# Attention, routing and experts on one core: rows transposed two jobs ahead into buffers of their own, fetched by SyncE; weight loads issued by ScalarE; low halves taken on VectorE

## The chip, the cores and the metric

One core of a Trainium2 chip. The metric is the device time of the whole program in microseconds (us). Three runs of the kernel before took 657.96 to 662.32 us, median 660.88 us. The profile is of one execution of 659.64 us, whose trace spans 657.9 us.

## The reference, cut to what matters

```
k_p, v_p = mean of 8 neighbouring keys / values           # 576 -> 72 per head
attn = softmax(q @ k_p.T / 8); x = (attn @ v_p) as [4608, 512]
logits = x @ w_gate;  e_idx = argmax(logits)              # one expert of 8 per row
gate_w = softmax(logits)[e_idx];  eom = sigmoid(x @ w_output_gate)
for e in range(8):
    out[rows of e] = gate_w * eom[:, e] * (relu(x[rows of e] @ w1[e]) @ w2[e])
```

w1[e] is 512 x 1024 and w2[e] 1024 x 512, all in fp32.

## The kernel before, in words

**Two halves.** The first half (to about 190 us) computes attention and routing, and scatters each row of x into a table `xs` in device memory that is ordered by expert. Its tail takes the first rows of expert 0 through the first layer (`hidden_chunk`, L613) and part of the second (`output_chunk`, L619). The second half (`experts`) runs the experts.

**Jobs and slots.** An expert's rows come in tiles (slots) of 128 rows. A job is 3 or 2 slots of one expert; an expert with a single tile has a job of 2 slots of which one is real (`single`, function `l1` with n = 0). How many jobs there are is read from a table at run time, so every engine runs the same nest (expert, trips of 3, pairs of 2) with `body` as its job. VectorE, ScalarE and GpSimd have it written out for all 8 experts (`loops`); TensorE has expert 0 written out and then a loop of 4 turns with two experts each (`looped`).

**Exact products.** An fp32 number is split into a high half (rounded) and a low half (the rest). x, the hidden layer and the weights are each held as high and low, and every product takes three matmuls. ScalarE takes each high half, and VectorE the low halves of the weights (`split`, L1059) and of the hidden layer (`low`, L1090). GpSimd takes the low half of x (`xl`, L1197).

**One job, engine by engine.** TensorE: first layer `l1` (8 chunks f of 128 hidden columns, 12 matmuls each, into 5 PSUM banks `p_h`, so chunk f waits until VectorE has read chunk f - 5), then second layer `l2` tile by tile into `p_y`. ScalarE: 4 DMAs that fetch the next job's rows (`fetch`, L860), then `hidden` (8 ReLUs, with a weight split behind some of them), then the high halves `xh` of the next job's rows (L979), then weight splits that are left (`rest`, `finish`). VectorE: the previous job's last output, `hidden`, then the transposes `turn` of the next rows in place in `xq` (L1047), then splits and the scaling of outputs `y` (L1079) in turn. GpSimd: `sc` and `dst` (gate values and output rows of the job), gathers of the row numbers two jobs ahead (`ahead`, L1180), `xl` of the next job's rows, then the scatters of the outputs (L1212). SyncE: the row fetch of job 1, then the 52 weight loads from m = 12 on (L884), each as soon as the piece that is 6 earlier in the ring `stage` has been split.

**What orders the next job's rows.** `xt`, the halves that TensorE reads, exists once: `xh` may begin when `l1` is over, and the next `l1` begins when `xl` is over (L913 in the code, semaphore `xl`). `xq` exists once too: the fetch of the next rows waits for `xl` of these.

**Weight splits.** Expert e + 1's pieces j = 4 to 7 (for e = 0 all 8) are split in e's first job, pieces j = 0 to 3 of e + 2 in e's last job (`plan`, `further`). In a first job each split stands behind one ReLU; in a job of one real tile two stand there (POS) and the rest after.

**Case of these inputs.** Expert 0 has jobs of 3, 3 and 2 slots (the first of them already begun in the first half), 1 a single tile, 2 one job of 3, 3 a pair, 4 has 3, 2 and 2, 5 has 3 and 3, 6 a single tile, 7 has 3, 3, 3 and 2: 16 jobs.

Of the kernel before, what the change touches and what calls it, by code (L numbers as in the profile page):

```python
# [22 lines left out]
P = 128  # L23
# [37 lines left out]
POS = (4, 6)  # L61

# [19 lines left out]
def attention_and_routing(ctx, tc, sh, qT, kT, v, wg, wst, xs):  # L82
# [599 lines left out]
def experts(st, nc, sh, wst, xs, out):  # L682
# [18 lines left out]
    names = ["l1", "tx", "l2", "xh", "xl", "hh", "hl", "y", "sc", "c", "x0", "x1", "x2", "t", "out", "wh", "wl", "on", "ad", "g", "pre", "xd", "x"]  # L701
# [149 lines left out]
    def fetch(eng, u, more, sem):  # L851
        def row(u):
            u = nc.s_assert_within(u, 0, R - 1, skip_runtime_bounds_check_because="there are at most 50 slots")
            return nc.values_load_multi_w_load_instructions(
                sh.at[0:1, bass.ds(u, 1)], [eng.engine], min_val=0, max_val=ZROW,
                skip_runtime_bounds_check_because="rows of the experts' tables")[1][0]

        def tiles(at, n):
            for h in range(4):
                eng.dma_start(xq[32 * h:32 * h + 32, 0:4 * n].bitcast(I32),  # L860
                              whole_rows(xs)[bass.ds(at, P * n), P * h:P * h + P].rearrange("(g t) f -> t g f", t=32)).then_inc(sem, LANDED // 4)

        with eng.If(more > 0):
            tiles(row(u), 3)
        with eng.Else():
            at, beside = row(u), row(u + 1)
            with eng.If(beside - at == P):
                tiles(at, 2)
            with eng.Else():
                tiles(at, 1)  # L870
# [3 lines left out]
    @blk.sync  # L874
    def _(eng):
        rows = table(eng)
        with eng.If(rows[E + 1] > 2):
            fetch(eng, WIDE, (counts(rows[0])[0] - 1) * 128 + (rows[0] & 128), q["xd"])
        for m in range(LOADED, 8 * E):
            if m == STAGES + EARLY:  # L880
                eng.wait_ge(q["xd"], LANDED)
            if m >= STAGES + EARLY:
                eng.wait_ge(q["wl"], m - STAGES + 1 - EARLY)
            eng.dma_start(sh.stage[m % STAGES], wst[m // 8][:, CHUNK * (m % 8):CHUNK * (m % 8 + 1)]).then_inc(LD[m % STAGES], 16)  # L884
# [88 lines left out]
    def _(eng):  # L973
        act = nc.scalar.activation

        def xh(u, k):
            _, turned, (high, _) = turned_rows(sh, k)
            eng.wait_ge(q["tx"], u + k + 1)
            act(high, turned, AF.Copy).then_inc(q["xh"], 1)  # L979

        def split(some):
            for e, j in some:
                m, s, hi, lo = piece(e, j)
                if m >= LOADED:
                    eng.wait_ge(LD[m % STAGES], 16 * ((m - LOADED) // STAGES + 1))
                act(hi, s, AF.Copy).then_inc(q["wh"], 1)  # L986

        def body(e, size, job, u, single, nth, more, last, late):
# [19 lines left out]
            def next_rows():  # L1008
                eng.wait_ge(q["xl"], u + size)
                fetch(eng, u + size, more, q["xd"])  # L1010

            if done is None:
                next_rows()
            else:
                with eng.If(done <= 0):
                    next_rows()
            eng.wait_ge(q["t"], ROWS)
            choose(eng, e, size, single, nth, hidden, hidden_one, split, done, late)
            xh(u + size, 0)
            xh(u + size, 1)  # L1020
            with eng.If(more > 0):
                xh(u + size, 2)
# [11 lines left out]
        with eng.If(rows[E + 1] <= 2):  # L1034
            fetch(eng, 0, rows[E + 1] & 1, q["x"])
        begin(eng, rows, ["xh", "hh"], lambda k: xh(0, k))
# [3 lines left out]
    def _(eng):  # L1040
        def turn(u, k, job):
            if isinstance(job, int):
                eng.wait_ge(q["x"], LANDED)
            else:
                eng.wait_ge(q["xd"], LANDED * job)
            x = turned_rows(sh, k)[0]
            nc.vector.transpose(x, x).then_inc(q["tx"], 1)  # L1047

        def turns(u, job, more):
            turn(u, 0, job)  # L1050
            turn(u, 1, job)
            with eng.If(more > 0):
                turn(u, 2, job)
# [31 lines left out]
        def body(e, size, job, u, single, nth, more, last, late):  # L1085
# [30 lines left out]
            def hidden_and_turns(some):  # L1116
                hidden(some)
                turns(u + size, job + 1, more)

            def turns_and_split(some):  # L1120
                turns(u + size, job + 1, more)
                split(some)

            if done is None:
                choose(eng, e, size, single, nth, hidden, hidden_one, split, done, late)
                turns(u + size, job + 1, more)
            else:
                choose(eng, e, size, single, nth, hidden_and_turns, None, turns_and_split, done, late)
            rest(eng, e, size, single, nth, split, 0, INIT + 1 if done is not None else 4, done, late)
            soon = SOON[size] if e else 0  # L1130
# [174 lines left out]
```

## Time and profile before

| | |
|---|---|
| median of 3 runs | 660.88 us (657.96 to 662.32) |
| the profiled execution | 659.64 us, of which its trace spans 657.9 us; mean granted clock 0.969 |
| TensorE (PE) busy | 593.5 us, 90% of the span |
| VectorE (DVE) busy | 351.0 us, 53% |
| ScalarE (ACT) busy | 262.6 us, 40% |
| GpSimd (POOL) busy | 286.6 us, 44% |
| moved by DMA | 100.97 MB, mean 153 GB/s |

Times in the rows are us from the span's start. A row of a timeline gives start, duration, engine, line, operation, output <- inputs and count; behind it, in brackets, the idle time of the engine just before and what ended it. "issue" there is a wait that ended with nothing that the profile shows. PEld is TensorE's weight load, SPq and ACTq are the queues that issue DMAs.

### The profile page before, as it was taken

The numbers are of one execution on the slowest core, as the hardware profiler recorded it, in microseconds if no ns is written. First come the engines' busy times: TensorE is split into PE (matmuls) and PEld (weight loads), VectorE is DVE, ScalarE is ACT, GpSimd is POOL, SyncE is SP. The second block draws the span as 40 slices with busy tenths as digits, with TensorE's granted clock in tenths as the row PEclk, the third lists the DMA queues.
The fourth block names the chain that finished last, engine by engine and source line by source line (L and its number), as shares of the span: only waits on it lengthen the run. The fifth ranks groups of instructions, "written<-read, shape, count | busy, mean of one in ns | idle before, by whom it ended". The sixth has DMA issues, their size and how long they took to land.

```text
span 657.9 us, 11957 instructions
## 1 busy us (share of the span) xinstructions
PE 593.5 (90%) x3543; PEld 539.7 (82%) x3544; DVE 351.0 (53%) x797; ACT 262.6 (40%) x694; POOL 286.6 (44%) x380
## 2 busy tenths in 40 slices
PE   0899999989894999879869999999999599999996
PEld 0798998878783989769668989989898498989895
DVE  5688899998767223577536513275135722222221
ACT  2788888787334212336334402154031411111110
POOL 3668889753626323255233324344231623223233
PEclk9999999999998899979969999999999889999998
DMA  8878889987468310648845710366105022111111
GB/s 257 271 221 291 289 293 348 331 279 243 173 173 302 94 47 31 211 134 252 228 132 162 235 57 28 88 139 213 58 12 146 29 63 62 43 49 39 36 37 40
DMA packets 48431, 100.97 MB, mean 153 GB/s; under 512 B 5931, under 2 KB 27819, under 8 KB 46432
## 3 DMA queue, kind: packets, MB, share of 16 engines
q1 hardware_dynamic: 22192, 66.64, 31.9%
q0 software_dynamic: 7792, 24.60, 11.1%
q10 hardware_dynamic: 18368, 8.92, 5.7%
q14 instruction: 59, 0.48, 0.3%
q8 instruction: 20, 0.33, 0.2%
HBM read 78.56 MB, written 25.49 MB: 158 GB/s over the span
## 4 chain that ended last, share of the span: by engine, by line
PE 61%; issue 3%; POOL 2%; DVE 2%; ACT 1%; DMA 1%; SPq 0%; DVEq 0%; POOLq 0%
PE p_h L922 33%; PE p_y L903 29%; POOL xt L1197 2%; DMA rows<-xs 1%; DVE w1b L1059 1%; DVE rows L1047 1%; DVE w2b L1059 0%; ACT w2a L986 0%; POOL rows L1180 0%; DVE rows L1079 0%; SPq L860 0%; DVE q_even L1103 0%; ACT xt L979 0%; ACT w2b L986 0%; POOL out L1212 0%
## 5 line engine op out<-in xcount | busy, mean ns | idle before, releaser
L994 ACT ACTIVATE ht<-p_h 128x384 fp32r<-128x384 f32 (+1 forms) x104 | 46.8, 450 | 270.0 <-PE p_h L922 269.9
L922 PE MATMUL p_h<-xt,w1b 128*128 128x384 f32 (+1 forms) x736 | 121.9, 329 | 16.8 <-issue 9.8
L922 PEld LDWEIGHTS p_h<-xt,w1b 128*128 128x128 f32 x736 | 120.6, 197 | 18.5 <-issue 18.0
L1090 DVE SCALAR_TENSOR_TENSOR ht<-p_h,ht 128x384 fp32r<-128x384 f32 (+1 forms) x104 | 52.6, 506 | 133.3 <-ACT ht L994 133.3
L903 PE MATMUL p_y<-w2b,ht 128*128 128x512 f32 x480 | 113.2, 396 | 0.0
L922 PE MATMUL p_h<-xt,w1a 128*128 128x256 f32 (+1 forms) x640 | 98.3, 316 | 13.3 <-POOL xt L1197 13.3
L922 PEld LDWEIGHTS p_h<-xt,w1a 128*128 128x128 f32 x640 | 97.4, 197 | 14.6 <-POOL xt L1197 9.2
L903 PEld LDWEIGHTS p_y<-w2b,ht 128*128 128x128 f32 x480 | 90.0, 188 | 21.0
L1212 POOL DMA_INDIRECT out<-rows,dst x41 | 41.5, 1013 | 123.1 <-DVE rows L1079 120.2
L903 PE MATMUL p_y<-w2a,ht 128*128 128x512 f32 x408 | 94.2, 390 | 0.4 <-PE p_y L619 0.4
L903 PEld LDWEIGHTS p_y<-w2a,ht 128*128 128x128 f32 x408 | 76.2, 188 | 16.3 <-issue 0.9
L1079 DVE TENSOR_SCALAR rows<-p_y,sc 128x512 f32<-128x512 f32 x41 | 30.4, 747 | 108.9 <-PE p_y L903 96.3
L1197 POOL TENSOR_TENSOR xt<-rows,xt 128x512 fp32r<-128x512 f32 x40 | 53.6, 1364 | 64.0 <-ACT xt L979 63.9
L261 ACT ACTIVATE p<-p_h,m 128x72 f32<-128x72 f32 x288 | 71.9, 373 | 21.9 <-DVE m L256 21.4
L278 PE MATMUL p_y<-vbd,pT 128*128 128x162 f32 (+1 forms) x480 | 74.0, 306 | 5.4 <-DVE xg L300 4.7
L278 PEld LDWEIGHTS p_y<-vbd,pT 128*128 128x128 f32 (+1 forms) x480 | 60.9, 179 | 9.0 <-DVE xg L300 4.1
L1180 POOL DMA_INDIRECT rows<-xs,src x51 | 54.6, 1071 | 24.7 <-POOL src L1176 14.3
L408 POOL DMA_INDIRECT xs<-xg,where x36 | 37.2, 1033 | 35.7 <-DVE grec L294 9.9
L191 POOL TENSOR_TENSOR kq<-kq 128x288 f32<-128x288 f32 (+1 forms) x63 | 40.6, 670 | 15.6 <-DMA kq<-kT 14.8
L250 PE MATMUL p_h<-kbd,q_even 128*128 128x144 f32 (+1 forms) x160 | 28.6, 306 | 15.4 <-DMA q_even<-qT 12.7
L271 ACT ACTIVATE pT<-ptr 128x384 f32<-128x384 f32 x72 | 38.7, 538 | 1.6 <-PE ptr L270 1.4
L270 PE MATMUL ptr<-ident,p 128*128 128x128 f32 x216 | 36.0, 276 | 1.0 <-DVE vbd L238 0.9
(165 smaller groups left out, 680.2 us busy)
## 6 DMA issues: line engine op xcount, KB each, us to landing
stage<-wst SPq DMA_DIRECT2D x64, 512.0 KB, 5.2
kq<-kT SPq DMA_DIRECT2D x7, 1152.0 KB
rows<-xs ACTq DMA_DIRECT2D x28, 192.0 KB
rows<-v SPq DMA_DIRECT2D x16, 288.0 KB
kq<-qT SPq DMA_DIRECT2D x4, 1152.0 KB
q_even<-qT SPq DMA_DIRECT2D x3, 1152.0 KB
xs<-xs SPq DMA_DIRECT2D x8, 320.0 KB
rows<-xs ACTq DMA_DIRECT2D x20, 128.0 KB
```

What stands on the lines that cost most here:

```text
L191: eng.tensor_tensor(k[:, :, 0:w], k[:, :, 0:w], k[:, :, w:2 * w], op=ALU.add)
L261: nc.scalar.activation(pt[i % 3][:, 4 * a + h, 0:KEYS], sv[:, h], AF.Exp, bias=m[:, h:h + 1])
L271: nc.scalar.activation(pT_t[i][:, 3 * a:3 * a + 3, :], tr[:, 0:384].rearrange("p (c n) -> p c n", c=3), AF.Copy)
L278: nc.tensor.matmul(av[r0:r0 + n, COLS * c:COLS * c + 2 * COLS], pT[:, 3 * a + c, r0:r0 + n], vbd[b % 2][:, a, c].rearrange("p h f -> p (h ...
L408: ins = nc.gpsimd.indirect_dma_start(out=whole_rows(xs), out_offset=bass.IndirectOffsetOnAxis(ap=where, axis=0), in_=x.bitcast(I32), in_of ...
L903: i = mm(to, ht[:, h, f, P * k:P * k + P], w[:, part, o:o + DM], start=(f == 0 and part == 0 and h == 0), stop=(f == 7 and h == 1))
L922: i = mm(to, w[:, part, o:o + P], x, start=(d == 0 and k == 0), stop=(d == 3 and k == len(terms) - 1))
L994: act(ht[:, 0, f, 0:size * P], p_h[f % DEEP][:, 0:size * P], AF.Relu).then_inc(q["hh"], 1)
L1090: nc.vector.scalar_tensor_tensor(ht[:, 1, f, 0:n], src, 0.0, ht[:, 0, f, 0:n].bitcast(F32), op0=ALU.max, op1=ALU.subtract).then_inc(q["hl" ...
L1180: nc.gpsimd.indirect_dma_start(out=xm[:, k].bitcast(I32), out_offset=None, in_=xs, in_offset=bass.IndirectOffsetOnAxis(ap=src[:, k:k + 1], ...
L1197: nc.gpsimd.tensor_tensor(low, turned, high.bitcast(F32), op=ALU.subtract).then_inc(q["xl"], 1)
L1212: nc.gpsimd.indirect_dma_start(out=out, out_offset=bass.IndirectOffsetOnAxis(ap=dst[:, k:k + 1], axis=0), in_=yb[2 if k == size - 1 else k ...
```

## The change

- Rows are transposed from `xq` into buffers `turned[0..2]` (two in SBUF, one in a PSUM bank that was the fifth of `p_h`; `l1` has 4 banks then). VectorE transposes for job j + 2 at the end of job j, ahead of `y`; always three tiles.
- SyncE fetches rows in a loop over all jobs of its own (`every_job`); the fetch of job j waits until the transposes of job j - 1 are done.
- ScalarE issues the weight loads: behind the split of piece m it waits until VectorE has split piece m - 2, and loads piece m + 4. It no longer fetches rows, and no longer waits for the row table (`t`) in each job.
- `xl` is VectorE's, behind `hidden`, in the second half and in `turn_x` of the first. All splits of a job and the transposes stand ahead of its `y`.

```
-        nc.gpsimd.tensor_tensor(low, turned, high.bitcast(F32), op=ALU.subtract)
+        nc.vector.tensor_tensor(low, turned, high.bitcast(F32), op=ALU.subtract)
...
-    p_h = sh.p_h + [psum(f"p_h{k}", [P, 512]) for k in (3, 4)]
+    p_h = sh.p_h + [psum("p_h3", [P, 512])]
+    turned = [sb(f"turned{k}", [P, 4, P], F32) for k in range(2)] + [psum("turned2", [P, 4, P])]
...
     @blk.sync
+            if job is not None:
+                eng.wait_ge(q["tx"], eng.to_reg(job * WIDE + 1))
+            for h in range(4):
+                eng.dma_start(xq[32 * h:32 * h + 32, 0:4 * n].bitcast(I32),
+                              whole_rows(xs)[bass.ds(row, P * n), P * h:P * h + P].rearrange("(g t) f -> t g f", t=32)).then_inc(q["xd"], LANDED // 4)
...
+            with eng.If(job > 0):
+                rows(job)
+                eng.wait_ge(q["t"], ROWS)
+            with eng.Else():
+                with eng.If(early > 0):
+                    eng.nop().then_inc(q["xd"], LANDED)
...
+        job, slot = every_job(eng, body)
+        for k in range(2):
+            fetch(slot, 1, job + k)
...
     @blk.scalar
         def split(some):
...
                 act(hi, s, AF.Copy).then_inc(q["wh"], 1)
+                if m - BEHIND >= EARLY and m - BEHIND + STAGES < 8 * E:
+                    eng.wait_ge(q["wl"], m - BEHIND + 1 - EARLY)
+                    load(m - BEHIND + STAGES)
...
-            def next_rows():
-                eng.wait_ge(q["xl"], u + size)
-                fetch(eng, u + size, more, q["xd"])
+            def begin_split(some):
+                split(some[:2])
+                next_high()
+                split(some[2:])
...
-            eng.wait_ge(q["t"], ROWS)
...
+        for m in range(LOADED, STAGES + EARLY):
+            load(m)
...
     @blk.vector
+        def xl(u, k):
+            eng.wait_ge(q["xh"], u + k + 1)
+            nc.vector.tensor_tensor(xt[:, 1, :, P * k:P * k + P], turned[k], xt[:, 0, :, P * k:P * k + P].bitcast(F32),
+                                    op=ALU.subtract).then_inc(q["xl"], 1)
+
+        def turn(k):
+            nc.vector.transpose(turned[k].rearrange("p d (g t) -> p g d t", g=4),
+                                xq[:, 4 * k:4 * k + 4].rearrange("p g (d r) -> p g d r", d=4)).then_inc(q["tx"], 1)
+
+        def turns(job, read=None, more=None):
+            if read is not None:
+                eng.wait_ge(q["xl"], read)
+            eng.wait_ge(q["xd"], LANDED * (job + 1))
...
             if done is None:
                 choose(eng, e, size, single, nth, hidden, hidden_one, split, done, late)
-                turns(u + size, job + 1, more)
+                next_low()
...
+            rest(eng, e, size, single, nth, split, 0, 99, done, late)
+            finish(eng, e, size, single, last, split, 0, 4)
+            turns(job + 2, u + size + 2, more)
             y(u, 0, job, done)
-            if done is not None:
+            if size == 3:
                 y(u, 1, job, done)
...
+        turns(1, 2, rows[E + 1] & 1)
...
     @blk.gpsimd
-            xl(u + size, 0)
-            xl(u + size, 1)
-            with eng.If(more > 0):
-                xl(u + size, 2)
```

## Rows read from the trace of the kernel before

**Rows 1.** The timeline of TensorE's matmuls in the second half; rows with an idle time before them, and ordinary ones to compare with.

```profile
212.72 19.21 PE L922 MATMUL p_h<-xt,w1a 128*128 128x384 f32 x96 [8.82 <-POOL xt L1197]
...
272.64 7.81 PE L922 MATMUL p_h<-xt,w1b 128*128 128x256 f32 x64 [1.92 <-issue]
...
290.78 19.41 PE L922 MATMUL p_h<-xt,w1a 128*128 128x384 f32 x96 [4.50 <-POOL xt L1197]
...
334.47 14.23 PE L922 MATMUL p_h<-xt,w1b 128*128 128x256 f32 x96 [7.93 <-issue]
...
359.74 16.80 PE L922 MATMUL p_h<-xt,w1a 128*128 128x384 f32 x96
...
525.53 20.00 PE L922 MATMUL p_h<-xt,w1b 128*128 128x384 f32 x96 [6.91 <-POOL xt L1197]
...
562.16 17.13 PE L922 MATMUL p_h<-xt,w1b 128*128 128x384 f32 x96
629.66 11.37 PE L922 MATMUL p_h<-xt,w1b 128*128 128x256 f32 x96
```

**Rows 2.** Stretches of the span: bounds, length, busy us (and instructions) of PE, PEld, DVE, ACT and POOL, then the granted TensorE clock, the DMA engines' busy share and GB/s.

```profile
212.70:217.00 4.30, 4.28 (x13) 4.28 (x14) 0.00 (x0) 0.03 (x1) 3.03 (x3) 0.50 0.78 262
270.70:272.60 1.90, 0.02 (x1) 0.00 (x0) 0.75 (x1) 0.00 (x0) 0.19 (x1) 1.00 1.04 343
272.60:286.30 13.70, 13.64 (x89) 12.17 (x89) 9.07 (x21) 6.09 (x14) 4.59 (x8) 1.00 0.62 212
```

**Rows 3.** The first wait: the chain that ended last, from the fetch of job 1's rows to its first matmul (start, us, what).

```profile
192.45 4.37 DMA rows<-xs
...
197.48 1.26 DVE rows L1047 x2
...
205.53 0.67 DVE rows L1079
```

**Rows 4.** The wait at 286.3: timelines of DVE, ACT and POOL.

```profile
283.43 0.28 DVE L1090 SCALAR_TENSOR_TENSOR ht<-q_even,ht 128x128 fp32r<-128x128 f32 x1
283.63 1.89 DVE L1047 STREAM_TRANSPOSE rows<-rows 128x512 f32<-128x512 f32 x3
287.17 5.70 DVE L1059 TENSOR_TENSOR w2a<-stage,w2a 128x1024 fp32r<-128x1024 f32 x2 [1.64 <-ACT w2a L986]
```

```profile
282.17 0.29 ACT L1002 ACTIVATE ht<-q_even 128x128 fp32r<-128x128 f32 x1
```

```profile
286.93 3.71 POOL L1197 TENSOR_TENSOR xt<-rows,xt 128x512 fp32r<-128x512 f32 x3
```

**Rows 5.** The wait at 518.6: timelines of DVE, POOL and PEld.

```profile
515.87 0.28 DVE L1090 SCALAR_TENSOR_TENSOR ht<-q_even,ht 128x128 fp32r<-128x128 f32 x1
519.60 3.46 DVE L1059 TENSOR_TENSOR w2b<-stage,w2b 128x1024 fp32r<-128x1024 f32 x2 [1.64 <-ACT w2b L986]
```

```profile
520.57 4.83 POOL L1197 TENSOR_TENSOR xt<-rows,xt 128x512 fp32r<-128x512 f32 x3
```

```profile
525.52 19.68 PEld L922 LDWEIGHTS p_h<-xt,w1b 128*128 128x128 f32 x96 [7.33 <-issue]
```

**Rows 6.** Instruction packets among the DMA traffic of four windows, in this order: 266 to 273, 286.2 to 287.6, 326 to 335 (q8 is the queue with 16 KB packets). In the windows 420 to 440 and 518.6 to 525.5 the answer has no row of q8.

```profile
q8 instruction: 1, 0.02, 1.0%
```

```profile
q8 instruction: 1, 0.02, 3.9%
```

```profile
q10 hardware_dynamic: 1231, 0.60, 29.9%
...
q8 instruction: 2, 0.03, 1.4%
```

**Rows 7.** Prices, from the answers by line: instructions, duration in ns (minimum/median/maximum), first and last start; for L884 also its DMAs' time to landing.

```profile
L884 SPq DMA_DIRECT2D stage<-wst x52: 327/328/423, 193.3 to 495.8; - x52
```

```profile
DMA to landing us min/median/max: 3.5/5.2/10.6
```

```profile
L860 ACTq DMA_DIRECT2D rows<-xs x60: 343/364/682, 214.2 to 621.6; - x60
```

```profile
L1059 DVE TENSOR_TENSOR w2a<-stage,w2a x12: 1211/1226/4567, 279.4 to 447.7; 128x1024 fp32r<-128x1024 f32 x12
```

```profile
L994 ACT ACTIVATE ht<-p_h x104: 383/491/493, 217.0 to 641.1; 128x384 fp32r<-128x384 f32 x64, 128x256 fp32r<-128x256 f32 x40
```

```profile
L1090 DVE SCALAR_TENSOR_TENSOR ht<-p_h,ht x104: 417/557/559, 217.5 to 641.5; 128x384 fp32r<-128x384 f32 x64, 128x256 fp32r<-128x256 f32 x40
```

```profile
L979 ACT ACTIVATE xt<-rows x40: 611/632/636, 199.6 to 643.2; 128x512 fp32r<-128x512 f32 x40
```

```profile
L1047 DVE STREAM_TRANSPOSE rows<-rows x40: 667/670/711, 196.8 to 642.5; 128x512 f32<-128x512 f32 x40
```

```profile
L1079 DVE TENSOR_SCALAR rows<-p_y,sc x41: 731/750/752, 205.4 to 652.3; 128x512 f32<-128x512 f32 x41
```

```profile
L986 ACT ACTIVATE w2a<-stage x12: 1040/1050/1054, 278.3 to 446.7; 128x1024 fp32r<-128x1024 f32 x12
```

**Rows 8.** The first half where the first rows are turned: timeline of DVE, then of PE.

```profile
160.19 0.68 DVE L440 TENSOR_TENSOR w1a<-stage,w1a 128x512 fp32r<-128x512 f32 x1
...
163.93 1.06 DVE L359 SCALAR_TENSOR_TENSOR grec__7_2311<-ez,gden 128x4 f32<-128x4 f32 x1
```

```profile
168.06 4.29 PE L613 MATMUL p_h<-xt,w1a 128*128 128x384 f32 x23 [1.15 <-POOL xt L448]
```

More of the change, by code (lines that the diff above doesn't have):

```diff
@@ L849, in skip, with every_job, whole @@
                 split(plan(e, 0) + further(e))
[L851 to L861, printed above, removed]
-        with eng.If(more > 0):
[L864 to L870, printed above, removed]
+    def every_job(eng, body):
+        job_r, slot_r = eng.alloc_register("job_r"), eng.alloc_register("slot_r")
+        eng.reg_mov(job_r, 0)
+        eng.reg_mov(slot_r, 0)
+        def whole(r, most):
+            return nc.s_assert_within(eng.snap(r), 0, most, skip_runtime_bounds_check_because="there are at most 50 slots")
+        with nc.Fori(0, E, engines=[eng.engine]) as g:
+            at = nc.s_assert_within(g, 0, E - 1, skip_runtime_bounds_check_because="experts in order")
+            v = nc.values_load_multi_w_load_instructions(
+                sh.table[0:1, bass.ds(at, 1)], [eng.engine], min_val=0, max_val=1023,
+                skip_runtime_bounds_check_because="counts of a few bits each")[1][0]
+            trips, pairs = counts(v)
+            for size, n in ((3, trips), (2, pairs)):
+                with eng.If(n > 0):
+                    job, slot = whole(job_r, 50), whole(slot_r, 56)
+                    with eng.Fori(0, n) as i:
+                        body(size, job + i, slot + i * size, v & 64)
+                    eng.reg_mov(job_r, job + n)
+                    eng.reg_mov(slot_r, slot + n * size)
+        return whole(job_r, 50), whole(slot_r, 56)
     blk = st.enter_context(nc.Block(no_gpsimd_drain=True))
@@ L1006, in body, with next_high @@
             done = started(e, size, rows, nth)
-            def next_rows():
-                eng.wait_ge(q["xl"], u + size)
-                fetch(eng, u + size, more, q["xd"])
+            def begin_split(some):
+                split(some[:2])
+                next_high()
+                split(some[2:])
+            def next_high():
+                xh(u + size, 0, job + 1)
+                xh(u + size, 1, job + 1)
+                with eng.If(more > 0):
+                    xh(u + size, 2, job + 1)
             if done is None:
-                next_rows()
-            else:
-                with eng.If(done <= 0):
-                    next_rows()
-            eng.wait_ge(q["t"], ROWS)
[L1018 to L1022, printed above, removed]
+                choose(eng, e, size, single, nth, hidden, hidden_one, split, done, late)
+                next_high()
+            else:
+                choose(eng, e, size, single, nth, lambda some: (hidden(some), next_high()), None, begin_split, done, late)
             rest(eng, e, size, single, nth, split, 0, 99, done, late)
@@ L1040, in _ @@
     def _(eng):
-        def turn(u, k, job):
-            if isinstance(job, int):
-                eng.wait_ge(q["x"], LANDED)
-            else:
[L1045 to L1053, printed above, removed]
+        def xl(u, k):
[9 more added lines that the diff above has]
+            eng.wait_ge(q["xd"], LANDED * (job + 1))
+            turn(0)
+            turn(1)
+            if more is None:
+                turn(2)
+            else:
+                with eng.If(more > 0):
+                    eng.wait_ge(q["xl"], read + 1)
+                    turn(2)
+                with eng.Else():
+                    turn(2)
         def split(some):
```

78 lines of the change are left out of this document (40 added, 38 removed).

## The prediction

> **What bounds the kernel now.** I read TensorE's own timeline first. From 190 us on its rows follow each other without a gap but for five waits [rows 1]. Three are put down to GpSimd's low half of x, L1197: 8.82 us to 212.72, 4.50 to 290.78, 6.91 to 525.53, together 20.2 us. Two have no releaser ("issue"): 1.92 us to 272.64 and 7.93 to 334.47. So in this half TensorE is the bound, and only what shortens these waits, or adds one, moves the end.
>
> Then the granted clock [rows 2]. After the wait to 212.72 TensorE works at 0.50 (the 1.2 GHz level) where it has 1.00 (2.4 GHz) elsewhere; the wait of 1.92 us did not lower it. What a lowered clock costs comes from two first layers of one shape [rows 1]: 19.21 against 16.80 us after the first wait (2.4), 19.41 against 16.80 after the second (2.6), 20.00 against 17.13 after the third (2.9). The three waits cost 20.2 + 7.9 = 28.1 us in all, which is the most that ending them can bring.
>
> Next, what ends each wait. At the first [rows 3], rows issued by 192.45 land at 196.8, and VectorE turns them until 198.74; it then splits weights and scales an output at 205.53 before GpSimd, which stands behind that output, comes to L1197. At the other two, VectorE's last low half of a one-tile job (283.43 to 283.71, 515.87 to 516.15) is followed by three transposes, the high halves, and three low halves on GpSimd [rows 4, 5].
>
> **The change, part by part.** *Low halves of x.* GpSimd loses 40 operations (three took 3.71 us [rows 4]). VectorE gains 40 operations of 128x512 with two inputs; the nearest row is the weight split of that size, 0.68 us [rows 8]; the ends are a low half of 384 columns, 0.557, and a split of twice the size, 1.226 [rows 7]. I take 0.68. *Transposes.* Always three tiles a job, 48 and more against 40, at 0.670; into another buffer or into PSUM they aren't shown, so 0.67 to twice that, and I take 0.67, as the count of elements is the same. They leave the path between two first layers. *Weight loads.* ScalarE gets 52 DMAs, at 0.328 (SyncE's price) to 0.364 us (its own for rows), and gives up 60 row DMAs at 0.364 [rows 7]: 17 to 19 us come and 22 go. Beside a ReLU (0.491) and the high half of a split (1.050) one such issue just fits into a chunk, 16.80 / 8 = 2.1 us. Loads have 4 pieces of lead instead of 6; in a first job a piece takes one chunk, so 8.4 us against a landing of 5.2 (at most 10.6) [rows 7]. Its new wait, for piece m - 2, has ReLUs queued behind it, and VectorE and TensorE's banks behind these; VectorE is less than two pieces behind, so it costs nothing, and if that cover goes, up to 1.2 us a piece. *Row fetch.* SyncE issues it when the transposes of the job before are done, a whole job ahead of need (at least 13 us, one-tile job) against a landing of 4.4 [rows 3]; nothing. SyncE's queue holds no other DMA then. *Four banks instead of five:* chunk 4 waits for VectorE's first low half; nothing in ordinary jobs, but it decides below.
>
> *First wait.* Let T be the end of job 1's transposes, 198.74 in the trace. SyncE's loop adds registers and branches before the fetch, and ScalarE's loads 12 and 13 (1 MB) go out before the rows and not behind them: 0 to 3 us, and I take T = 200. Then VectorE does two splits (2.4) and three low halves (2.0) [rows 7, 8]: TensorE starts at T + 4.5 = 204.5 (it is out of work at 212.72 - 8.82 = 203.9) against 212.72. But VectorE also has six splits (7.3), three transposes (2.0) and three outputs (2.2) before the first low half of the hidden layer (0.56): T + 16.6 = 216.6. TensorE is at chunk 4 at 204.5 + 8.4 = 212.9 and waits 3.7 us; four chunks more end its first layer at T + 25 = 225.0, where it ended at 212.72 + 19.21 = 231.9. That is 6.9 us, less a lowered clock, if a wait of 3.7 us lowers it: 1.92 did not, 4.50 did. I take 5.5, within 2 (T = 202, clock lowered) and 8.2 (T = 198.74).
>
> *Second wait.* ScalarE's last ReLU ends at 282.46 [rows 4], perhaps 1.2 us later with two loads and their waits in the job; high halves (0.632 each [rows 7]) and low halves follow at once, the last low half at about 286.5, when TensorE is just out of work (290.78 - 4.50 = 286.28). But there is something behind L1197. In the stretch 286.2 to 287.6 an instruction packet of 16 KB comes over q8, as one does around the wait of 1.92 us and two in the wait of 7.93, and none where experts change without a gap [rows 6]. So I leave 1.9 us: 4.5 - 1.9 + 2.6 (clock) = 5.2, within 4 and 7.1. VectorE must be at job 4's first low half by TensorE's chunk 4, 288.2 + 8.4 = 296.6; it has low halves (2.0), two splits (2.5), transposes (2.0) and two outputs (1.5) from 284.4 on, so 292.9: in time.
>
> On this the trace has a row to weigh: the two splits at 287.17 took 5.70 us, one of them 4.567, against 1.226 each, while GpSimd ran L1197; at 519.60 two took 3.46 beside L1197 [rows 4, 5, 7]. With GpSimd's share gone I count them at 1.226. The Trainium skill, SBUF — State Buffer, section "SBUF: two separate sides", says that VectorE with two SBUF inputs and GpSimd take a shared port pair in turn, the loser waiting for a whole instruction; the trace agrees (4.567 against 1.226). By that rule the sum stands with 3.7 us to spare. Were the long splits of another cause and to stay, VectorE would be 3.3 us later, at 296.3 with 0.3 to spare, and the second wait would give as much or, with one late load, some 2 us less.
>
> *Third wait.* The last low half ends at 516.15, three low halves later it is 518.3, and TensorE is out of work at 525.53 - 6.91 = 518.62; no instruction packet here [rows 6]. All of it goes: 6.9 + 2.9 = 9.8, I take 9.7 and 8 as the lower end.
>
> *First half.* The same move adds three low halves to VectorE. It waits for ScalarE's high half (0.63) before each low half, three times: 0.7 of waiting and 0.68 of work each. Against that, an operation of 128x4 elements took 1.06 us beside GpSimd's low half [rows 8], and GpSimd's third low half was what TensorE waited for at 168.06. I count +0.7 us, between 0 and +3.
>
> *The two waits without a releaser* stay: 1.92, and 7.93 with its lowered clock (14.23 against 11.37, 2.9).
>
> **Sum:** 659.64 - 5.5 - 5.2 - 9.7 + 0.7 = 639.9, say **640 us**. The profiled execution is 1.24 us under the median of the runs; I don't add that.
>
> **The rivals.**
>
> *A: VectorE becomes the bound (0.15).* Its order puts low halves, splits and transposes ahead of outputs and the next job's low halves. If transposes cost double, T comes at 202 and each one-tile job leaves VectorE some 2 to 4 us late, the first wait gives 2.8, the second 1.4 (a new wait at chunk 4, clock lowered), the third 6.8: 659.64 - 11.0 + 0.7 = 649. For it: VectorE is busy 9.07 of the 13.70 us of a one-tile job already [rows 2]. Against it: the next job's chunk 4 comes 8.4 us after its start, and VectorE has only to be there by then.
>
> *B: the wait of 7.93 us goes too (0.12).* Two instruction packets come in it, while rows (0.60 MB on q10) fill the DMA engines [rows 6]. Weight loads now go out some 3 us earlier there, and the stretch may be emptier. From a part to all of 7.93 + 2.9: 629 to 636. The Trainium skill, Runtime: NRT & Kernel Launch, section "Instruction fetch mechanics", says that a taken branch to a page not held stalls until a DMA has fetched it, which fits a stall whose length is that of the DMA queue; the trace agrees in its packets.
>
> *C: the change does not end the waits (0.08).* TensorE's weight load names "issue", not L1197, before 525.52 [rows 5], so the releaser could be an instruction fetch. The empty q8 at 518.6 speaks against it. Then only the first wait shrinks: 659.64 - 5 = 655.
>
> *D: rows come late (0.06), slower than before.* VectorE's wait for the fetched rows stands ahead of its outputs and of all that follows in order. The place is each change of expert, where the fetch meets a burst of four weight loads. Rows still moved 0.60 MB in the window 326 to 335 [rows 6], so a fetch can stretch to some 9 us. [...] Seven changes at 3 + 2.7 us are 40, less the 20 gained: 680.
>
> The forecast itself has 0.59.
>
> **Range and chances.** A measurement of this kernel tells about 1% (6.6 us) from no change. Bounds of the forecast: gains of 2 + 4 + 8 - 3 = 11 at worst, 8.2 + 7.1 + 9.8 = 25 at best, the ends being unlikely together: 632 to 647. A reaches to 649 and B to 629; I take 630 to 650, which leaves out C, D and the ends. Faster by over 1%: forecast, A and B, 0.86; same: C, 0.08; slower: D, 0.06.
>
> **What would show it.** Right: no L1197, and first layers at 525 and 290 (less what came before) without an idle row and at about 17 us; VectorE's 40 new operations at 0.68; a wait of some 3 to 4 us inside job 1's first layer, released by VectorE. Wrong: an idle row before the transposes released by the row DMA (D), transposes well over 0.67 (A), the wait before expert 3 short (B), or first layers of experts 2 and 7 that still wait (C).

## The result and the profile after

The changed kernel takes 633.71 us (median of 4 runs, 630.31 to 635.89) against 659.88 us (657.96 to 662.32) for the kernel before on the same chip: ratio 0.960 [0.954, 0.966]. That is faster, as forecast, inside the range of 630 to 650 and 6.3 us below the forecast of 640.

The profiled execution took 630.31 us, the fastest of the four, and its trace spans 628.6 us with a mean granted clock of 0.988. The page's list of busy times shows work moved from GpSimd (286.6 us before, 234.2 now) to VectorE (351.0 before, 371.7 now); TensorE is busy for 94% of the span (90% before):

```profile
PE 587.8 (94%) x3543; PEld 533.9 (85%) x3544; DVE 371.7 (59%) x851; ACT 260.5 (41%) x693; POOL 234.2 (37%) x337
```

TensorE's timeline in the second half. These rows answer to [rows 1]; an idle row before a matmul is again in brackets:

```profile
190.26 7.76 PE L620 MATMUL p_y<-w2a,ht 128*128 128x512 f32 x33 [0.99 <-PEq L1318]
202.00 8.06 PE L933 MATMUL p_y<-w2a,ht 128*128 128x512 f32 x24 [3.98 <-DVEq L1160]
209.90 16.83 PE L952 MATMUL p_h<-xt,w1a 128*128 128x384 f32 x96
...
266.56 7.81 PE L952 MATMUL p_h<-xt,w1b 128*128 128x256 f32 x64 [1.05 <-issue]
...
280.04 16.84 PE L952 MATMUL p_h<-xt,w1a 128*128 128x384 f32 x96
...
316.06 13.02 PE L952 MATMUL p_h<-xt,w1b 128*128 128x256 f32 x96 [2.82 <-issue]
...
498.96 17.23 PE L952 MATMUL p_h<-xt,w1b 128*128 128x384 f32 x96
```

The two waits of the one-tile jobs (4.50 and 6.91 us) have no idle row any more, and the first layers behind them take 16.84 and 17.23 us where they took 19.41 and 20.00. A wait of 3.98 us at 202.00 is new: it stands ahead of the last 24 matmuls of job 0, not ahead of job 1, and its releaser is VectorE's queue. The waits marked "issue", 1.92 and 7.93 us before, are 1.05 and 2.82 us now.

Where the profiled executions differ is read from the ends of these rows (start + length), each counted from the row at 190.26, which answers to the one at 189.98 before:

| to the end of | before | after | gain of the stretch | forecast |
|---|---|---|---|---|
| first half | 189.98 | 190.26 | -0.3 | -0.7 |
| job 1's first layer | 231.93 | 226.73 | 5.5 | 5.5 |
| the first matmul behind the 1.92 wait (its start) | 272.64 | 266.56 | 0.9 | 0 |
| the first layer at the second wait | 310.19 | 296.88 | 7.2 | 5.2 |
| expert 3's first layer | 348.70 | 329.08 | 6.3 | 0 |
| the first layer at the third wait | 545.53 | 516.19 | 9.7 | 9.7 |
| sum | | | 29.3 | 19.7 |

29.3 us is the difference of the spans (657.9 - 628.6). The medians differ by 26.2; the 3 us between these two are not placed. The first half alone ended anywhere from 190.0 to 194.7 us in the profiles of this study, also where its code was that of before, so this much lies within its own variation. For that reason single executions are compared below by their **second half**, from that first row to the end of the span: 467.9 us before, 438.3 after.

The prices that had been bounds now have rows of their own, in the answers by line (instructions, then minimum/median/maximum in ns):

```profile
L1080 DVE TENSOR_TENSOR xt<-turned,xt x40: 683/686/694, 204.5 to 614.1; 128x512 fp32r<-128x512 f32 x40
L1084 DVE STREAM_TRANSPOSE turned<-rows x51: 667/684/712, 200.5 to 616.1; 128x512 f32<-128x512 f32 x51
L1106 DVE TENSOR_TENSOR w2a<-stage,w2a x12: 1215/1224/1227, 273.3 to 428.1; 128x1024 fp32r<-128x1024 f32 x12
L1012 ACTq DMA_DIRECT2D stage<-wst x52: 333/334/506, 190.1 to 473.9; - x52
```

A low half of x costs VectorE 0.686 us (0.68 taken), a transpose into the new buffers 0.684 (0.67 taken, up to twice feared), a load on ScalarE's queue 0.334 (0.328 to 0.364). The longest weight split is 1.227 us; before it was 4.567 [rows 7].

### The profile page after: what moved, and what is told of

It reads as the page before. It is cut to its first block, busy times and chain, and to the rows that moved or that the text cites. A ratio compares the mean times of both kernels' runs of the same rounds, so it can differ in the third digit from the quotient of the medians.

```text
span 628.6 us, 12115 instructions
## 1 busy us (share of the span) xinstructions
PE 587.8 (94%) x3543; PEld 533.9 (85%) x3544; DVE 371.7 (59%) x851; ACT 260.5 (41%) x693; POOL 234.2 (37%) x337
## 4 chain that ended last, share of the span: by engine, by line
PE 66%; issue 1%; DMA 1%; SPq 0%; POOL 0%; DVE 0%; DVEq 0%; POOLq 0%
PE p_h L952 33%; PE p_y L933 33%; DMA rows<-xs 1%; SPq L890 0%; POOL out L1253 0%; DVE rows L1126 0%; PE p_y L985 0%; SPq L884 0%; SPq L863 0%; DVE turned L1084 0%; SPq L870 0%; SPq L907 0%; SPq L903 0%; SPq L868 0%; SPq L861 0%
## 5 line engine op out<-in xcount | busy, mean ns | idle before, releaser
L952 PE MATMUL p_h<-xt,w1b 128*128 128x384 f32 (+1 forms) x736 | 117.9, 321 | 3.9 <-issue 3.9
L952 PEld LDWEIGHTS p_h<-xt,w1b 128*128 128x128 f32 x736 | 116.6, 191 | 5.5 <-issue 5.1
L933 PE MATMUL p_y<-w2a,ht 128*128 128x512 f32 x408 | 96.5, 397 | 4.0 <-DVEq L1160 4.0
L933 PEld LDWEIGHTS p_y<-w2a,ht 128*128 128x128 f32 x408 | 77.9, 192 | 20.6 <-issue 4.4
L952 PE MATMUL p_h<-xt,w1a 128*128 128x256 f32 (+1 forms) x640 | 93.3, 306 | 0.0
L952 PEld LDWEIGHTS p_h<-xt,w1a 128*128 128x128 f32 x640 | 92.7, 190 | 0.7 <-issue 0.2
L1230 POOL DMA_INDIRECT rows<-xs,src x51 | 56.0, 1098 | 24.6 <-POOL src L1226 14.3
L272 ACT ACTIVATE pT<-ptr 128x384 f32<-128x384 f32 x72 | 38.3, 531 | 2.6 <-PE ptr L271 1.3
L251 PEld LDWEIGHTS p_h<-kbd,q_even 128*128 128x128 f32 (+1 forms) x160 | 23.0, 192 | 16.1 <-issue 12.6
```

Of the source, the lines that this page charges most:

```text
L251: nc.tensor.matmul(s[r0:r0 + n, 144 * c:144 * c + 144], q_t[b][:, 2 * a + c, s0:s0 + n], kbd[b % 2][:, 2 * a + c, :], start=True, stop=True)
L272: nc.scalar.activation(pT_t[i][:, 3 * a:3 * a + 3, :], tr[:, 0:384].rearrange("p (c n) -> p c n", c=3), AF.Copy)
L933: i = mm(to, ht[:, h, f, P * k:P * k + P], w[:, part, o:o + DM], start=(f == 0 and part == 0 and h == 0), stop=(f == 7 and h == 1))
L952: i = mm(to, w[:, part, o:o + P], x, start=(d == 0 and k == 0), stop=(d == 3 and k == len(terms) - 1))
L1230: nc.gpsimd.indirect_dma_start(out=xm[:, k].bitcast(I32), out_offset=None, in_=xs, in_offset=bass.IndirectOffsetOnAxis(ap=src[:, k:k + 1], ...
```

## The experiments

After the result three things were open: which part of the change ended GpSimd's three waits; why the wait before expert 3 shrank, which had been left at 7.93 us; and what the wait at 202.00 costs. In the expectations L is the theory that the wait before expert 3 is an instruction fetch of TensorE held up by weight loads on the DMA engines; the others are named where they stand.

**1. The low halves alone.** The kernel before, with `xl` in the second half moved from GpSimd to VectorE, behind the transposes; fetch, loads and buffers as before.

```
     @blk.vector
+        def xl(u, k):
+            _, turned, (high, low) = turned_rows(sh, k)
+            eng.wait_ge(q["xh"], u + k + 1)
+            nc.vector.tensor_tensor(low, turned, high.bitcast(F32), op=ALU.subtract).then_inc(q["xl"], 1)
...
+            xl(u + size, 0)
+            xl(u + size, 1)
...
     @blk.gpsimd
-            xl(u + size, 0)
-            xl(u + size, 1)
...
```

> The kernel before with one part of the change: in the second half VectorE takes the low halves of x, behind the transposes (and in job 0 behind five splits); everything else as before. Theory M (the waits were GpSimd's low halves, 3.7 us and more each time, and its queue): the wait to 290.78 shrinks from 4.50 to about 0.7 us (transposes 1.9, last high half, one low half of 0.69 end at 287.0 against 286.3), or to 1.9 if an instruction packet stands behind it; the wait to 525.53 from 6.91 to about 0.7; the first from 8.82 to about 3; clock losses of some 2.5 us each go with them. Time about 638 us (ratio 0.966). Rival R (the transposes ahead are what ended the waits): at least half of these waits stay, 648 us or more. The wait of 7.93 us before expert 3 stays by both.

Measured: 640.40 us (637.86 to 641.49), ratio 0.970 [0.966, 0.975]. TensorE's timeline:

```profile
208.85 18.50 PE L922 MATMUL p_h<-xt,w1a 128*128 128x384 f32 x96 [2.67 <-DVE xt L1052]
...
269.41 7.73 PE L922 MATMUL p_h<-xt,w1b 128*128 128x256 f32 x64 [3.28 <-issue]
...
284.18 16.91 PE L922 MATMUL p_h<-xt,w1a 128*128 128x384 f32 x96 [1.20 <-DVE xt L1052]
...
322.98 14.32 PE L922 MATMUL p_h<-xt,w1b 128*128 128x256 f32 x96 [5.53 <-issue]
...
508.47 17.22 PE L922 MATMUL p_h<-xt,w1b 128*128 128x384 f32 x96 [1.25 <-DVE xt L1052]
```

This one part brings 659.81 - 640.40 = 19.4 us of the 26.2. At the one-tile jobs 4.50 becomes 1.20 and 6.91 becomes 1.25 (0.7 was expected), with the first layers behind them as short as ordinary ones (16.91 and 17.22 us). What stays there is the transposes' share: VectorE turns three tiles between the last low half of one job and the first of the next, and 1.2 us of that shows. That is about what turning them ahead is worth at each one-tile job. By the second halves the whole change is 445.9 - 438.3 = 7.6 us ahead of this version: 1.3 behind it at the end of job 1's first layer (36.5 us against 35.1 from the second half's first row), 3.6 gained up to the end of the first layer at the second wait (1.2 of it this gap, 2.2 the wait of 1.05 us after, which is 3.28 here), 4.0 before expert 3 and 1.3 at the third wait. One thing was not expected: the wait before expert 3, which was to stay, fell from 7.93 to 5.53 us, although SyncE issues the weight loads here as before; experiment 6 comes back to it.

**2. The weight loads alone.** The kernel before, with the loads issued by ScalarE as in the change; rows, transposes and `xl` untouched.

```
     @blk.sync
-        for m in range(LOADED, 8 * E):
...
-            eng.dma_start(sh.stage[m % STAGES], wst[m // 8][:, CHUNK * (m % 8):CHUNK * (m % 8 + 1)]).then_inc(LD[m % STAGES], 16)
...
     @blk.scalar
         def split(some):
...
+                if m - BEHIND >= EARLY and m - BEHIND + STAGES < 8 * E:
+                    eng.wait_ge(q["wl"], m - BEHIND + 1 - EARLY)
+                    load(m - BEHIND + STAGES)
...
```

> The kernel before with another part alone: ScalarE issues the weight loads behind its splits (piece m, wait for VectorE's piece m - 2, load m + 4); rows are fetched, transposed and halved as before. Theory L (the wait before expert 3 was 7.93 us because weight loads, late in the burst, filled the DMA engines when TensorE fetched instructions): it shrinks to 3 to 5 us, the time to about 655 us (ratio 0.993); the three waits on GpSimd stay as they were (4 to 9 us). Rival: the loads are not the cause (it is the row fetch, or where the code lies): the wait stays at 7 to 9 us and the time at 658 to 661 us; if ScalarE suffers from issuing, ReLUs come late and first layers with splits get longer than 17 us.

Measured: 657.66 us (655.02 to 660.64, 10 runs) against 659.81, ratio 0.996 [0.993, 0.999].

```profile
216.79 19.46 PE L917 MATMUL p_h<-xt,w1a 128*128 128x384 f32 x96 [8.15 <-POOL xt L1201]
...
296.79 18.74 PE L917 MATMUL p_h<-xt,w1a 128*128 128x384 f32 x96 [5.03 <-POOL xt L1201]
...
335.44 12.77 PE L917 MATMUL p_h<-xt,w1b 128*128 128x256 f32 x96 [3.56 <-issue]
...
525.06 19.20 PE L917 MATMUL p_h<-xt,w1b 128*128 128x384 f32 x96 [6.93 <-POOL xt L1201]
```

GpSimd's three waits stay, and the wait before expert 3 is 3.56 us instead of 7.93. So moving the loads shortens that one. It does not isolate them: in this execution ScalarE also fetched its rows later, 1.1 us after TensorE was out of work (332.95 against 331.88) and not 5.0 us ahead (321.51 against 326.54), so rows and loads both left that stretch; experiment 6 comes back to this too. By the median the loads are worth some 2.2 us by themselves, a third of a per cent. Against their gain stand two new waits of TensorE for VectorE in the one-tile job, 0.89 and 0.66 us.

**3. The release ahead of the wait.** In the changed kernel VectorE's sign that job 0's first output bank is free (semaphore `y`) is an instruction of job 0's `body`, and so stands behind `turns(1)`, which waits for job 1's rows. TensorE's last 24 matmuls of job 0 need it. Here it stands ahead.

```
         rows = table(eng)
         eng.nop().then_inc(q["tx"], 1)
+        eng.nop().then_inc(q["y"], 1)
...
             with eng.If(job > 0):
                 last_output(u)
-            with eng.Else():
-                eng.nop().then_inc(q["y"], 1)
```

> The changed kernel, but the release of the first output bank (one semaphore increment of VectorE in job 0) stands ahead of its wait for job 1's rows, not behind it. The 3.98 us wait of TensorE to 202.00 goes, by both theories, and job 1's first layer starts at about 206.5 and not 209.9. Theory V (VectorE's row of work in job 0 is the bound): a new wait of 2 to 3 us at chunk 4 of that layer, its end at about 226 as now, time within 1 us of the changed kernel's 633.7. Rival (the misplaced release alone costs): no wait at chunk 4, the layer ends at about 223.3, 3.4 us less, 630 us.

Measured: 634.54 us (633.63 to 635.97), ratio 0.962 [0.958, 0.967], no gain over the changed kernel.

```profile
199.38 5.78 PE L933 MATMUL p_y<-w2a,ht 128*128 128x512 f32 x24 [0.43 <-PE p_y L620]
207.25 8.60 PE L952 MATMUL p_h<-xt,w1a 128*128 128x384 f32 x48 [2.09 <-DVE xt L1080]
219.31 10.15 PE L952 MATMUL p_h<-xt,w1a 128*128 128x384 f32 x48 [3.46 <-DVE ht L1137]
```

The 24 matmuls run at once and at full speed (5.78 us, not 8.06), and TensorE then waits in two other places for VectorE: 2.09 us for the low half of x and 3.46 us at chunk 4, the wait that had been forecast. What TensorE saves early it gives back, because the row of work on VectorE ends no earlier: the first low half of the hidden layer starts 27.5 us after the second half's first row, and 26.7 with the late release. The difference is a wait inside that row, for ScalarE's high half of a weight piece, which in turn had waited 1.38 us for its load:

```profile
213.81 1.23 DVE L1106 TENSOR_TENSOR w2b<-stage,w2b 128x1024 fp32r<-128x1024 f32 x1 [0.94 <-ACT w2b L1019]
```

In this execution job 1's first layer ended 38.3 us after the second half's first row (36.5 with the late release).

**4. Loads behind the rows.** Experiment 3, with ScalarE's loads 12 and 13 behind the landing of job 1's rows, to see whether they slow the rows.

```
+                eng.wait_ge(q["xd"], 2 * LANDED)
+                for m in range(LOADED, STAGES + EARLY):
+                    load(m)
...
```

> As the run before this one, and ScalarE's first two weight loads (1 MB) stand behind the landing of job 1's rows instead of ahead of them. Theory (rows landed at 200.46 and not 196.84 for two reasons: SyncE issues 2.1 us later, and 1.5 us of sharing the DMA engines with the loads): the rows land about 1.5 us earlier, at 199, and all that follows from VectorE too: 1.5 us less than the run before this one. Rival: sharing costs nothing, rows land at 200.4, and the loads of pieces 12 and 13 come late, so the time is the same or up to 2 us more.

Measured: 635.06 us (634.24 to 636.71), ratio 0.964 [0.959, 0.968]: no gain over experiment 3 (634.54). From the issue to the end of landing the rows took 7.13 us (194.93 to 202.06), against 7.42 in experiment 3 (193.83 to 201.25) and 7.57 in the changed kernel (192.89 to 200.46). With one execution of each, the difference that can be put down to sharing with the loads is 0.3 us, a fifth of what had been expected. Before, the rows took 6.07 us (190.77 to 196.84); why they take 1.1 to 1.5 us longer in these three stays open.

**5. A shorter row of work on VectorE.** Experiment 3, and: SyncE fetches job 1's rows ahead of its loop, and three of the weight splits that VectorE has between the rows and the first hidden chunk (pieces 5 to 7 of expert 1) are done behind ReLUs of job 1. The program then needs expert 0 to have at least two jobs of three, as here.

```
+                    with eng.If(done == 0):
+                        many(plan(e, 0)[INIT:AHEAD[3]])
...
-            some = plan(e, 0)[max(j0, INIT):min(j1, AHEAD[3])]
-            if some:
-                with eng.If(done > 0):
-                    split(some)
+            pass
...
     @blk.sync
...
+        with eng.If(early > 0):
+            eng.nop().then_inc(q["xd"], LANDED)
...
+                fetch(WIDE, 3)
```

> The changed kernel with three edits to its first wait: the release of the first output bank ahead of the wait for rows; SyncE's fetch of job 1's rows ahead of its loop; and three of the eight weight splits of job 0 (all pieces of it stay, for both ScalarE and VectorE) moved behind ReLUs of job 1. It needs expert 0 to have two jobs of three tiles, which it has here. Theory V (VectorE's row of work from the landing of the rows to the first low half of the hidden layer, T + 15, is the bound): fetch issued about 1.5 us earlier, low half at T + 12.9, so no wait at chunk 4, and job 1's first layer ends at 222 to 223 and not 226.7: 4 us less than the changed kernel, about 629.5 us. Rival (another wait takes its place, as a late weight or the outputs): within 1.5 us of the changed kernel.

Measured: 627.17 us (626.80 to 630.39), ratio to the kernel before 0.953 [0.946, 0.959]. The changed kernel itself ran again on this chip:

> The changed kernel once more, on the same chip as the three runs before it: 633.7 us, 630 to 636.

It took 631.97 us (630.83 to 632.51), ratio 0.958 [0.951, 0.964]; all four runs of the new version lie below all four of the changed one, and the medians differ by 4.8 us (0.8%). TensorE's timeline of the new version:

```profile
199.85 5.74 PE L943 MATMUL p_y<-w2a,ht 128*128 128x512 f32 x24 [0.43 <-PE p_y L620]
207.28 16.91 PE L962 MATMUL p_h<-xt,w1a 128*128 128x384 f32 x96 [1.69 <-DVE xt L1090]
...
313.53 13.03 PE L962 MATMUL p_h<-xt,w1b 128*128 128x256 f32 x96 [3.08 <-issue]
```

With the release early and the row shorter, the 24 matmuls run at full speed, a wait of 1.69 us is left ahead of job 1, and there is none at chunk 4. The two edits of the row were not run apart, but the traces show their shares. The fetch is issued 1.7 us earlier than in the changed kernel on this chip (0.92 against 2.63 us after the second half's first row), and yet the rows land only 0.6 us earlier (9.61 against 10.18): from issue to landing they take 8.69 us here. VectorE's first low half of the hidden layer starts 4.0 us earlier (22.65 against 26.65), so some 3.4 of these come from the three splits.

**6. The wait before expert 3: code or traffic.** Four variants of the changed kernel, each of them run once. The first has 128 more empty instructions on TensorE, behind the output chunks, which move its code on:

> The changed kernel with 128 no-operations in TensorE's program behind the first half's leftover matmuls, where it waits 4 us anyway: all of its later code lies 128 instructions further on. It tells why the wait before expert 3 is 2.82 us and was 7.93. Theory L (the jump back of the loop fetches two 16 KB packets, and how long that takes hangs on the load of the DMA engines): the place of the code doesn't matter, the wait stays at 2 to 4 us. Rival P (the changed kernel's code merely lies better against the blocks that are fetched): the wait changes by more than 3 us or goes. The time is within 3 us of the changed kernel's, apart from the no-operations.

It took 631.69 us. The wait is 3.49 us, against 2.82 and 3.27 in the two profiles of the changed kernel, and TensorE's work behind it is unchanged (12.96 us). Moving the code by this much does next to nothing. The second has 2 MB of useless loads behind the row fetch of job 7:

> The changed kernel with 2 MB of loads from device memory to device memory, of no use, issued by SyncE once, right behind the row fetch of job 7, some 3 to 5 us before the wait before expert 3. Theory L: the two instruction packets come later, and the wait grows from 2.82 to 5 to 9 us, with a lowered clock behind it; time 3 to 8 us more, 637 to 642 us. Rival P: wait 2.8 us as before, time 634 to 636 us.

It took 633.97 us. The wait is 3.12 us, but the traffic began at 314.07, only 0.8 us before the first instruction packet (314.84): it came too late to tell anything. So in the other two SyncE issues it ahead of each row fetch of two tiles (`n == 2`; fetches of one tile have none), once 4 MB in pieces of 4 KB, as the weight loads have them, and once 1.5 MB in pieces of 512 bytes:

```
+                if n == 2:
+                    for c in range(8):
+                        eng.dma_start(junk[bass.ds(job * P, P), CHUNK * c:CHUNK * c + CHUNK], wst[c][:, 0:CHUNK]).then_inc(q["du"], 16)
```

> The run with useless traffic began its traffic only 0.7 us before TensorE's first instruction packet, too late to tell. Here SyncE issues 4 MB of useless loads (device memory to device memory, 4 KB rows) ahead of the row fetch of each job of at most two tiles, so also ahead of job 7's, some 4 to 6 us before that packet. In the runs so far the first of the two packets starts 2.2 to 2.8 us before TensorE is out of work in the changed kernel and its variants, 1.9 before in the loads-only run, 0.2 after in the low-halves-only run and 2.5 after in the kernel before; TensorE goes on 5.2 to 6.1 us after it in all. Theory L (a backlog on the DMA engines delays the first packet): it starts at or after TensorE's last matmul, the wait before expert 3 is 5 to 9 us. Rival: it starts 2 to 3 us before, the wait stays at 2.8 to 3.5. Rows of some jobs come late in this run, so its whole time says little.

> As the run before this one with 1.5 MB of useless traffic in pieces of 512 bytes, like the row fetch's. Theory L with the small packets as the cause: the wait before expert 3 is 5 to 9 us here, and more than with the 4 KB rows; without: 2.8 to 3.5 us. The whole time says little.

They took 658.08 and 642.80 us. TensorE's timeline with the 4 KB pieces:

```profile
231.10 10.61 PE L956 MATMUL p_h<-xt,w1a 128*128 128x384 f32 x48 [11.92 <-DVE ht L1141]
...
311.93 11.09 PE L956 MATMUL p_h<-xt,w1a 128*128 128x384 f32 x48 [7.52 <-DVE ht L1141]
...
344.83 12.95 PE L956 MATMUL p_h<-xt,w1b 128*128 128x256 f32 x96 [5.46 <-issue]
```

and with the 512-byte pieces:

```profile
328.56 13.02 PE L956 MATMUL p_h<-xt,w1b 128*128 128x256 f32 x96 [2.87 <-issue]
```

The wait grows with the 4 KB pieces (5.46 us) and not with the small ones (2.87). What happens in between is seen in the DMA view (queue: packets, MB, share of 16 engines), in a short window that holds the first of the two 16 KB instruction packets of q8. Before, 328.8 to 329.2; TensorE had been out of work since 326.54:

```profile
q8 instruction: 1, 0.02, 16.7%
```

After, 310.3 to 310.7, while TensorE still had work until 313.24:

```profile
q8 instruction: 1, 0.02, 18.9%
```

With the 4 KB pieces, 338.9 to 339.3, as TensorE ran out of work at 339.37:

```profile
q8 instruction: 1, 0.02, 22.9%
```

| kernel | first packet, from TensorE's end of work | next matmul, from that packet | wait |
|---|---|---|---|
| before | +2.5 | 5.5 | 7.93 |
| low halves alone (1) | +0.2 | 5.4 | 5.53 |
| loads alone (2) | -1.9 | 5.4 | 3.56 |
| changed | -2.7 | 5.6 | 2.82 |
| changed, again | -2.8 | 6.1 | 3.27 |
| more code (6) | -2.7 | 6.1 | 3.49 |
| 4 KB pieces (6) | -0.3 | 5.7 | 5.46 |
| 512-byte pieces (6) | -2.4 | 5.3 | 2.87 |

In all of them TensorE goes on 5.3 to 6.1 us after the first packet; what differs is when that packet comes. The second packet does not decide it: with the 4 KB pieces it started at 345.25, after TensorE had gone on at 344.83.

What moved in the 5 us before the end of work is read from the queues. q1 is SyncE's queue and q10 ScalarE's, so q1 has the weight loads before, and the rows and the useless traffic in the changed kernel and its variants. Before (321.5 to 326.5) q1 moved the weight loads, and with the 4 KB pieces (334 to 339) the useless ones:

```profile
q1 hardware_dynamic: 292, 1.07, 78.5%
```

```profile
q1 hardware_dynamic: 293, 1.09, 80.8%
```

In the changed kernel (308 to 313) q1 moved rows, in pieces of 512 bytes, and on q10 the weight loads had already gone out:

```profile
q1 hardware_dynamic: 1088, 0.52, 40.7%
...
q10 hardware_dynamic: 9, 0.02, 1.2%
```

So the rows alone don't hold the packet back: 0.52 MB of them moved there, and it came early all the same. Theory L also fits experiment 1, where q1 still moved 1.02 MB of weight loads (312.45 to 317.45) and the packet came 0.2 us after the end of work; why it was not as late there as before is not shown.

So the wait is that of an instruction fetch that starts late where large loads are still moving: theory L fits the table, and one execution with traffic added (-0.3 us, against -2.8 to -2.2 in the other profiles of the changed kernel and its variants) supports it as a cause. What about the loads holds the packet back is not shown. The two runs with traffic differ in its amount (4 MB and 1.5 MB) as well as in the size of the pieces, and in the three runs where the packet came at about the end of work or later the large pieces were on SyncE's queue.

## Why the prediction was right, and where not

**Right: what ended the waits of the one-tile jobs.** GpSimd's low halves made them, experiment 1 shows it by moving these alone; the third wait gave the 9.7 us forecast. Rival C (they don't end) is out.

**Right: VectorE has the room.** Rival A fell with its price: 0.684 us a transpose, not double. The long split of 4.567 us is gone with GpSimd's operation beside it (at most 1.227 now), as the prediction had read it from [rows 4, 5, 7].

**Right in size, wrong in mechanism: the first wait.** It gave the 5.5 us forecast, by another road, so that the number agrees is luck. Job 1's rows landed at 200.46 and were turned at 202.37, not at T = 200, which is where the lower end of 2 us had been put. And a step was missing: where the change adds a wait to VectorE's stream, what stands behind it includes not only splits and low halves but the release of TensorE's output bank. VectorE's timeline shows it, with 5.13 us of idle time ahead of the transposes:

```profile
200.46 1.91 DVE L1084 STREAM_TRANSPOSE turned<-rows 128x512 f32<-128x512 f32 x3 [5.13 <-DMA rows<-xs]
202.28 2.35 DVE L1106 TENSOR_TENSOR w1b<-stage,w1b 128x1024 fp32r<-128x1024 f32 x2
204.55 1.89 DVE L1080 TENSOR_TENSOR xt<-turned,xt 128x512 fp32r<-128x512 f32 x3
206.35 2.35 DVE L1106 TENSOR_TENSOR w1b<-stage,w1b 128x1024 fp32r<-128x1024 f32 x2
208.62 4.62 DVE L1106 TENSOR_TENSOR w2b<-stage,w2b 128x1024 fp32r<-128x1024 f32 x4
213.16 1.91 DVE L1084 STREAM_TRANSPOSE turned<-rows 128x512 f32<-128x512 f32 x3
214.98 2.03 DVE L1126 TENSOR_SCALAR rows<-p_y,sc 128x512 f32<-128x512 f32 x3
216.92 1.48 DVE L1137 SCALAR_TENSOR_TENSOR ht<-p_h,ht 128x384 fp32r<-128x384 f32 x3
```

The row of work is the one forecast, and a little shorter: its first low half of the hidden layer starts at 216.92, 14.6 us after the transposes end, where T + 16.6 for the end of that low half (0.56) had meant 16.0. TensorE began late, so it was not at chunk 4 before this was done; with the release moved (experiment 3) the forecast wait is there, 3.46 us against 3.7, though 0.94 us of VectorE's lateness there is the wait for ScalarE that was not forecast. And a shorter row (experiment 5) ends the layer 32.5 us into the second half instead of 35.8 in the changed kernel on that chip.

**Wrong: "the two waits without a releaser stay".** This is the step that failed. The wait before expert 3 went from 7.93 to 2.82 us and its first layer from 14.23 to 13.02: 6.3 us in all, and the wait of 1.92 gave 0.9. The trace had shown the two packets and rows on q10 [rows 6], and rival B had said that the stretch "may be emptier" with earlier loads. It was given 0.12, and it named the rows as what fills the DMA engines; the runs point to the weight loads that were still moving when TensorE came to the end of the expert (1.07 MB in the 5 us before), and the change hands these out earlier. The wait of 1.92 us has the same shape with one packet: before, the packet started 1.7 us ahead of TensorE's end of work (269.03, 270.72), after, 2.4 us ahead (263.06, 265.50), and TensorE went on 3.6 and 3.5 us after it. The Trainium skill, Runtime: NRT & Kernel Launch, section "Instruction fetch mechanics", says that a taken branch to a page that is not held waits for a DMA to bring it; the packets and the waits behind them fit that (5.3 to 6.1 us from packet to matmul in the table), and the table shows besides that this DMA can itself be late.

**Wrong by 2 us: a leftover at the second wait.** 1.9 us were kept for an instruction packet. The packet that came in that wait before (at 286.41, 0.1 us after TensorE was out of work) has its counterpart, by the order of the packets, at 281.67 in the changed kernel, 1.6 us after the next first layer had begun, and no wait was left. So this layer can begin without it. The error was to take a packet in a wait for its cause: before, packets of q8 come also while TensorE works without a gap, as at 274.92, 279.63 and 312.70.

**Sum of the miss,** by the two profiled executions: 639.9 - 630.3 = 9.6 us = 6.3 (expert 3) + 2.0 (second wait) + 0.9 (the wait of 1.92) + 0.4 (first half).

**Rival D** did not occur, but the 4 KB pieces of experiment 6 made it: with the rows that late, VectorE reached the hidden layer late, TensorE waited 11.92 and 7.52 us at chunk 4, and the kernel took as long as before (658.08 us). Its place had been put at each change of expert; in that run it came at the first layers of jobs 1 and 4.

## What to carry to other kernels

Before a wait is added or moved up in an in-order engine, list every semaphore that it raises further on, not only its arithmetic: the one that another engine needs first sets the price. A wait without a releaser, with instruction packets in it, calls for a count of what the DMA engines move just before it: handing large loads out earlier shortened one from 7.93 to 3.56 us with no other edit (experiment 2). And where several engines pass a tile on between two products, first move the step of the slowest: here it was 19.4 of 26.2 us (experiment 1).

## What had not been expected of the hardware

The same length of idle time does not always lower TensorE's clock. After the wait of 2.82 us before expert 3 the granted clock fell (0.57 on average from 316.06 to 320.00) and the layer took 13.02 us, against 11.37 at full speed [rows 1]; experiment 1 has a wait of 3.28 us with the work behind it at full speed (granted clock 1.00 from 269.41 to 277.10; 7.73 us, against 7.81 in [rows 1]). In the rows of before a wait of 1.92 us had not lowered it and one of 4.50 had; between the two the length alone does not tell. How the two waits differ for the chip stays open.

The wait of 3.98 us at 202.00 lowered the clock too, for the 24 matmuls behind it. The rows are windows of the changed kernel (bounds, length, busy us of PE, PEld, DVE, ACT and POOL, granted clock, DMA share, GB/s):

```profile
202.00:209.90 7.90, 7.90 (x25) 6.28 (x26) 7.90 (x10) 5.88 (x7) 5.76 (x5) 0.69 0.82 223
209.90:218.00 8.10, 8.10 (x48) 8.10 (x47) 8.10 (x12) 2.83 (x5) 1.85 (x3) 1.00 0.77 289
```

So its price, 2.3 us (8.06 against 5.74), was paid in the second layer of job 0, and job 1's first layer ran at 1.00 throughout.
